# One explicit order of all TensorE units, scores, values and transposes in a fused attention and GEGLU kernel

## The chip, the cores and the metric

The kernel runs on one core of a Trainium2 chip. A core has five engines that work side by side: TensorE (PE, matrix products, with PEld for its weight loads), VectorE (DVE), ScalarE (ACT), GpSimd (POOL, which here issues the loads and casts them) and SyncE (SP, which issues stores and transposing transfers). The metric is the device time of the program in microseconds (us); the median of three runs of the kernel before is 404.07 us (403.4 to 404.55). The profile is of one execution, and its span runs from the first to the last instruction.

## The reference

Eight batches of 12 heads, 448 positions, 64 numbers a head: an attention with squared ReLU in place of the softmax, then a GEGLU block over the 3584 rows of 768 numbers that come out.

```python
scores = np.matmul(q, k.transpose(0, 1, 3, 2)) / np.sqrt(64)
attn = np.maximum(scores, 0.0) ** 2 / 448
x = np.matmul(attn, v)                    # to rows: (8 * 448, 12 * 64)
g, val = x @ w_gate, x @ w_val            # 768 -> 1536
out = (0.5 * g * (1 + erf(g / sqrt(2))) * val) @ w_out    # 1536 -> 768
```

## The kernel before

**Tiles.** The array is used as four tiles of 64 x 64. Each product is cut along its contraction in two: the lower half of it (operations named PE0 in the code) runs in one half of the array, the upper (PE1) in the other, and both add into the same bank of PSUM, one behind the other. So while one unit's upper half runs, the next unit's lower half runs beside it. A step is two matmuls of 64 rows and 64 columns over 448, 384 or 224 columns (`mm`, L365).

**Units.** A *score unit* (`add_scores`) makes two key chunks' scores in PSUM; ACT takes their ReLU (tile `rl`), and DVE squares two units at a time (`attnT`). A *value unit* (`add_values`, `ff<-attnT,v`) makes two heads' attention; DVE or ACT copies it to `xT`. A *gate* or *value product* (`add_gate_value`, `ff<-xT,wg` and `ff<-xT,wv`) makes 128 columns of the first FFN layer; ACT takes the gelu, DVE multiplies (`uT`). Part of the columns of batches 1 to 7 is made by seven products in place of eight, by Strassen's scheme as Winograd has it, as *pairs* (`add_pair`, over the sums `ts` of tokens and `ws` of weights, the latter made on DVE by `add_pair_sums`). The second FFN layer is done likewise for groups of rows (`add_product`, over `uT`, sums `s` of it, and sums `wt` of weights). *Transposes* of queries and keys are done on PE for batches 0 and 1 (`add_transposes`), and for batches 2 to 7 by a DVE copy (`qkr`) and two transposing transfers on SP for each third of a batch (`add_dma_transposes`).

**What sets the order.** The kernel is planned while it is built. `run_plan` takes the operations of every engine with a cost in us and what they wait for, and appends the next one that can start. Batch 0's attention has its own order (`START`), and everything on PE behind that start stands in a list of units sorted by a place in time (`later`). `next_unit` looks at the first 40 of them and takes the first that can start at once, or else the one that can start soonest; a score unit may also start inside another unit's run. ACT, DVE and SP take whatever is ready by priority. The order of each engine in the program is what comes out; the chip then runs each engine in order, with semaphores between them.

`LINE` gives the sequence of the FFN units: a digit is the next gate or value product of that batch, `2A6` is the product 6 of pair A of batch 2, `d7` is product 7 of row group d. The attention of batches 1 to 7 is not in it: each batch's score units, values and transposes are spread evenly between two places in time, which come from where the batch's FFN begins and two numbers a batch in `SHIFT`. The sums of pair weights go behind the last product that a rule names.

**Buffers that matter.** Scores use two bank pairs of PSUM at first; from a point on (`WIDE`) one is given to the FFN, and every score unit waits for the ReLU of the unit ahead of it. Loads of queries, keys and values on POOL wait for ReLUs and copies of earlier thirds (`PACE`), so they follow the order of scores. Transposing transfers wait for a mark in PE's order, one for each 256 PE instructions (`Blocks`, `gate`); stores behind row group 8 keep away from the edges of these blocks (`hold`).

Of the kernel before, what the change touches and what calls it, by code (L numbers as in the profile page):

```python
# [11 lines left out]
LINE = """  # L12
0 0 0 0 0 0 0 0 0 0 0 0 0 0 0 0 0 0 0 0 0 0 0 0 1 1A1 1 2 1A6 2 2 1 1A7 1A2 1A5 2 a1 2 a2 2A1 1A4 1
1 1 1A3 1 2 1 2A2 a6 1 2A7 a7 2 1 a5 1 1 2A6 2 2 1 1 1 1 a3 1 1 a4 1 1 b1 b7 c1 b2 b6 2A4 2 c6 b4 b5
c7 c5 2B1 2B6 c4 2B2 c3 b3 2A5 2 c2 2B7 2B4 2B5 2A3 2 3A1 2 3A2 2 2B3 2 2 3A6 3A7 d7 d1 3B1 d2 4C1
3B2 3 3C1 3B7 3 d6 3 e1 d4 3C7 3 3C6 3 3B6 e7 3B4 e6 3A4 3A5 3 3 3 3C2 3 3B5 3 3 d5 3C4 3A3 3C5 d3
4A1 4C2 3B3 3C3 e5 3 4A7 f1 f2 f6 e4 f7 4C7 4 e2 4C6 4A2 e3 g7 4B1 f5 4B6 4 4A6 4B2 g1 4B7 4 g2 4A5
4C5 4A4 4B4 4B5 f4 4D7 4D1 4C4 4 5B1 5 4D6 4D5 4A3 4 g6 4 g5 4C3 4B3 f3 4 5 5B2 4D2 4D4 g3 4D3 5C1
g4 5B6 5B7 5C2 5B5 5A1 4 5A6 5 5C7 5A7 5A2 5 5B4 5D1 h1 5A4 5D6 5D2 h6 5C6 h7 5 5D7 5D5 5A5 6A1 5B3
5 5C5 5C4 5A3 5C3 5D4 6B1 5 5D3 5 6A2 6B2 h4 i1 i2 6B7 6A6 i7 h5 6A7 h2 6D1 6F7 6D7 h3 j1 6D6 6C1  # L20
6D2 i6 j7 6E1 j6 6C7 6C2 6E7 i5 i4 6C6 6B6 6A5 6A4 6E6 6A3 6F1 6B4 6B5 6C5 6D5 6D4 6F6 i3 6B3 6F5
6C4 j5 6D3 6E2 6F2 6E5 6F4 6C3 6F3 6E4 6E3 7E7 j2 7E1 7B1 k1 k7 7E2 7A1 7B2 7B7 k2 7B6 7E6 j4 7C1 k6
7A2 l7 7C7 7C6 7A7 7B4 7C2 l1 7B5 7B3 k5 7A6 7F1 j3 7D1 7E5 7F7 7F2 7A5 k4 7F6 7E4 l6 7D7 7C4 7D2
7F4 7D6 7D5 7D4 7D3 l2 7F5 7A4 7C5 7C3 7E3 7A3 l5 l4 7F3 m1 n1 m7 k3 l3 m2 m6 n6 m5 n7 n4 m3 n5 n2
m4 n3
"""
# [5 lines left out]
"""  # L32


SHIFT = "-183 -79.5 40.75 1.75 -343.75 -112 43.75 -179.5 27.25 -513.5 -447.25 0.25"

# [59 lines left out]
class Unit:  # L96


    def __init__(self, at, los, his, box=None, closer=None, prev=None):
        self.at, self.los, self.his, self.box, self.closer, self.prev = at, los, his, box, closer, prev  # L100
        self.begun = False
        self.short = False


AHEAD = 40
BANK = 0.3


def run_plan(queues, pools, units, banks, arrivals, together, fill, blocks, span):

# [47 lines left out]
    def next_unit(short):  # L158
        best = None
        now = max(free["PE0"], floor)  # L160
        for u in units[:AHEAD]:
# [16 lines left out]
            if u.box is not None:  # L178
                k, end = None, None
                for n, c in banks.items():  # L180
                    x = 0.0 if c is None else c.end
                    if x is not None and (end is None or x < end):
                        k, end = n, x
                if k is None:
                    continue
                t = max(t, end + BANK)
            if short and t > now:
                continue
            t = max(t, now)
            if best is None or t < best[0]:  # L190
                best = (t, u, k)
                if t <= now:
                    break
# [5 lines left out]
    while left:  # L199
# [33 lines left out]
        if isinstance(op, tuple):  # L233
            _, u, k = op
            u.begun = True
            units.remove(u)
            if k is not None:
                u.box["k"] = k
                banks[k] = u.closer()
            queues["PE0"][at["PE0"]:at["PE0"]] = u.los  # L240
            pools["PE1"] += u.his
            op = u.los[0]
# [34 lines left out]
def kernel(  # L277
# [60 lines left out]
    mpool = ctx.enter_context(tc.tile_pool(name="mpool", bufs=RING_M))  # L338
    loaded = tc.tile_pool(name="lpool", bufs=2), tc.tile_pool(name="hpool", bufs=RING_H)
    lpool, hpool = (pool.__enter__() for pool in loaded)  # L340
# [125 lines left out]
    def add_dma_transposes(b, m, deps=()):  # L466
# [22 lines left out]
        n = len(regrouped)  # L489
        copy = Op("DVE", 0.62, emit_copy, [wait, *(regrouped[n - 2] if n > 1 else ())], lag=0.15, prio=1)  # L490
        DVE.append(copy)
# [93 lines left out]

    def then(at, step, los, his, box=None, closer=None):

        if not isinstance(at, list) and at > FIXED:
            his[0].deps.append(los[-1])
            for i, op in enumerate(his[1:]):  # L590
                op.after = his[i]
            later.append(Unit(at, los, his, box, closer))
            return
# [283 lines left out]
    def first_use(i):  # L877

        return min(b for b in range(B) if NPB[b] > i)
# [280 lines left out]
    def add_product(at, gr, name, final):  # L1160
# [103 lines left out]
        then(at, RS, *ops, box if name in opens else None, lambda: st["read", stages_last[stage]])  # L1264

# [36 lines left out]


    work = []
    flow = [[("g", b, fc, g) for fc in range(2 * NPB[b], FC) for g in range(2)] for b in range(B)]
    line = []
    for x in LINE.split():
        if len(x) == 1:
            line.append(flow[int(x)].pop(0))
        elif len(x) == 3:  # L1310
            line.append(("7", int(x[0]), "ABCDEFGHIJKL".index(x[1]), x[2]))
        else:
            line.append(("p", "abcdefghijklmn".index(x[0]), x[1]))
    assert not any(flow)
    at = 0.0
    starts = [None] * B
    placed = []
    for item in line:
        if item[0] == "g" and starts[item[1]] is None:
            starts[item[1]] = at  # L1320
        if item[0] == "7" and starts[item[1]] is None:
            starts[item[1]] = at
        placed.append((at, item))
        at += {"g": G, "7": G / 2, "p": R}[item[0]]
    starts.append(at)
    WIDE = 20.0
    for at, item in placed:
        if item[0] == "g":
            work.append((at, 5, add_gate_value, item[1:]))
        elif item[0] == "7":  # L1330
            work.append((at, 5, add_pair, item[1:]))
        else:
            _, gr, name = item
            work.append((at, 5, add_product, (gr, name, gr == B * SC // 4 - 1)))
    LEAD = 6.0

    LO1 = 2.0
    for b in range(B):
        if b == 0:
            lo, hi = -60.0, -12.0  # L1340
        elif b == 1:
            lo, hi = LO1, starts[1] - LEAD
        elif b == 2:
            lo, hi = starts[1] + 8.0, starts[2] - LEAD
        else:
            lo, hi = starts[b - 1] - LEAD, starts[b] - LEAD
        if b >= EARLY:
            lo, hi = lo + float(SHIFT.split()[2 * (b - 2)]), hi + float(SHIFT.split()[2 * (b - 2) + 1])
        if b >= EARLY:
            lo = max(lo, passed)  # L1350
            hi = max(hi, lo + 1.0)
        passed = hi
        step = (hi - lo) / NU
        if b < EARLY:
            for m in range(NM):
                for rs in ((0,), (1,)) if b == 0 else ((0, 1),):


                    x = -5.0 if m else -2.0
                    t_at = placed0[f"t{m}{rs[0]}"] if b == 0 else lo + SC * m * step + x  # L1360
                    if (b, m) == (1, 0):
                        t_at = PLACE5 + 0.05
                    work.append((t_at, 1, add_transposes, (b, m, rs)))
        for pr in range(NPAIR):
            u = SC * (pr // 2) + (VC - 1, SC - 1)[pr % 2]
            x = lo + u * step + max(4.5, 2.5 * step)
            if b == 0:
                x = placed0[f"v{pr}"] if pr < NPAIR - 1 else PLACE5
            work.append((x, 2, add_values, (b, pr)))
# [3 lines left out]
    for i in reversed(range(max(NPB))):  # L1373
        behind = [n for n, w in enumerate(work) if w[2] is add_gate_value and w[3][0] == first_use(i) - 1][-1]
        work.insert(behind + 1, (0.0, 5, lambda at, i: add_pair_sums(i), (i,)))


    for at, _, fn, args in work:
        fn(at, *args)
# [84 lines left out]
    banks = {k: readers.get(k, [None])[-1] for k in range(FB + 2)}  # L1464
    run_plan({"PE0": PE0, "POOL": POOL}, {"PE1": PE1, "ACT": ACT, "DVE": DVE, "SP": SP, "IDLE": IDLE}, later,
             banks, arrivals, ("PE0", "PE1"), fill, blocks, BLOCK)

# [29 lines left out]
```

## Time and profile before

| what | us |
|---|---|
| median of three runs (lowest, highest) | 404.07 (403.4, 404.55) |
| span of the profiled execution | 394.9 |
| outside the span (404.07 - 394.9) | 9.2 |
| PE busy, and 40 to 60 us into the span | 386.3, 20.00 of 20 |
| ACT busy | 258.7 |
| DVE busy | 309.6 |
| ReLU of one score unit on ACT | 0.919 |

The profiled execution has no time of its own beside its span, so the median stands for it. A row of instructions reads: line, engine, operation, out<-in by the program's names, shape, count, then busy time and mean time of one, then the engine's idle time ahead of them and what ended it. Idle time is given to the releaser that came last. PE's ends are modelled and its matmuls overlap, so that "busy" says only that some step was running.

### The profile page before, as it was taken

Reading aid. Unit: us, or ns where it says so; the run is one execution under the profiler, and the core shown is the slowest. Engines: PE = TensorE matmul, PEld = TensorE weight load, DVE = VectorE, ACT = ScalarE, POOL = GpSimd, SP = SyncE. Lnnn points to the kernel's source line nnn. Section 1 sums busy time; section 2 is a strip of 40 time slices with the busy share of each in tenths; the row PEclk is TensorE's granted clock in tenths of the full one; section 3 lists DMA queues with packets and bytes.
Section 4 is the critical chain, followed back from the end, with each engine's and each line's share of the span. In section 5 each row is a group of like instructions: output and inputs, shape, how many; then the busy total and the mean of one; then the engine's idle time right before and its main releaser. Section 6 shows DMA issues by size and latency. Waiting matters only on the chain.

```text
span 394.9 us, 22904 instructions
## 1 busy us (share of the span) xinstructions
PE 386.3 (98%) x10570; PEld 358.4 (91%) x10573; DVE 309.6 (78%) x522; ACT 258.7 (66%) x401; POOL 97.2 (25%) x156
## 2 busy tenths in 40 slices
PE   7999999999999999999999999999999999999995
PEld 3458889999999999999999999989999999999994
DVE  3885779968797499999797779758988999866772
ACT  5866872357677767787786478765787886535541
POOL 7656523322233323232332123310211000000000
PEclk9999999999999999999999999999999999999999
DMA  8999999988999969887999598880763501121134
GB/s 110 186 199 199 197 209 185 112 103 83 161 148 175 152 85 143 93 132 121 113 148 108 124 122 111 139 83 11 103 105 56 125 6 43 45 45 45 43 85 120
DMA packets 85567, 45.12 MB, mean 114 GB/s; under 512 B 46048, under 2 KB 82400, under 8 KB 85472
## 3 DMA queue, kind: packets, MB, share of 16 engines
q0 software_dynamic: 46944, 24.39, 49.9%
q1 hardware_dynamic: 37888, 18.49, 26.4%
q8 instruction: 82, 1.34, 1.4%
q10 hardware_dynamic: 640, 0.79, 0.6%
q14 instruction: 13, 0.11, 0.1%
HBM read 48.76 MB, written 11.01 MB: 151 GB/s over the span
## 4 chain that ended last, share of the span: by engine, by line
PE 93%; DVE 2%; DMA 2%; POOL 1%; issue 1%; ACT 0%; ACTq 0%; POOLq 0%
PE ff L365 85%; PE sp L365 7%; DMA qk<-in_k_dram 2%; DVE attnT L728 1%; PE sp L646 1%; POOL qk L424 1%; DVE xT L792 0%; PE ff L646 0%; ACTq L1241 0%; ACT osb L1225 0%; ACT rl L714 0%; PE ff L567 0%; DVE osb L1223 0%; DVE qkT L650 0%; POOL ident masks.py:199 0%
## 5 line engine op out<-in xcount | busy, mean ns | idle before, releaser
L714 ACT ACTIVATE rl<-sp 128x896 bf16<-128x896 f32 x168 | 152.1, 919 | 50.4 <-PE sp L365 45.1
L365 PE MATMUL ff<-xT,wg 64*64 64x224 bf16 (+1 forms) x2304 | 183.7, 299 | 0.6 <-issue 0.6
L365 PEld LDWEIGHTS <-wv 64*64 64x64 bf16 x2304 | 127.7, 107 | 4.4
L365 PEld LDWEIGHTS <-wg 64*64 64x64 bf16 x2304 | 123.3, 107 | 5.0 <-issue 0.5
L365 PE MATMUL ff<-xT,wv 64*64 64x448 bf16 x1056 | 120.8, 349 | 0.0
L728 DVE TENSOR_TENSOR attnT<-rl 128x1792 bf16<-128x1792 bf16 (+1 forms) x98 | 92.2, 952 | 6.6 <-ACT rl L714 6.2
L365 PEld LDWEIGHTS <-ws 64*64 64x64 bf16 x1872 | 92.3, 107 | 1.4 <-issue 1.0
L365 PEld LDWEIGHTS <-s 64*64 64x64 bf16 x1344 | 81.6, 107 | 1.8
L365 PE MATMUL ff<-attnT,v 64*64 64x448 bf16 (+1 forms) x768 | 79.7, 326 | 0.7 <-DVE attnT L728 0.6
L365 PE MATMUL ff<-ts,wv 64*64 64x224 bf16 x1248 | 78.7, 256 | 0.0
L365 PE MATMUL ff<-ts,ws 64*64 64x224 bf16 x1248 | 77.6, 256 | 0.0
L365 PE MATMUL sp<-qkT 64*64 64x448 bf16 (+1 forms) x768 | 74.6, 328 | 0.7 <-issue 0.3
L365 PE MATMUL ff<-wo,s 64*64 64x384 bf16 x672 | 63.4, 323 | 0.0
L966 DVE TENSOR_TENSOR part<-ff,part 128x448 f32<-128x448 f32 x78 | 47.5, 622 | 20.1 <-PE ff L365 16.4
L365 PEld LDWEIGHTS <-uT 64*64 64x64 bf16 x1008 | 62.5, 107 | 0.7
L365 PE MATMUL ff<-wt,s 64*64 64x384 bf16 x672 | 61.4, 322 | 0.0
L365 PE MATMUL ff<-wo,uT 64*64 64x384 bf16 x672 | 60.7, 322 | 0.0
L962 ACT COPY part<-ff 128x448 f32<-128x448 f32 x78 | 41.3, 534 | 12.4 <-PE ff L365 11.2
L443 POOL DMA_DIRECT2D v<-in_v_dram x48 | 29.6, 620 | 80.3 <-ACT rl L714 44.3
L365 PEld LDWEIGHTS <-v 64*64 64x64 bf16 x768 | 44.7, 107 | 4.1 <-issue 1.7
L424 POOL DMA_DIRECT2D qk<-in_q_dram x43 | 27.6, 642 | 80.0 <-ACT rl L714 59.5
L1049 DVE TENSOR_TENSOR uT<-gel,ff 128x448 bf16<-128x448 bf16 x44 | 27.3, 620 | 22.4 <-PE ff L365 11.0
(51 smaller groups left out, 423.9 us busy)
## 6 DMA issues: line engine op xcount, KB each, us to landing
out_dram<-osb SPq DMA_DIRECT2D x48, 192.0 KB, 3.3
v<-in_v_dram POOLq DMA_DIRECT2D x48, 128.0 KB, 4.1
wg<-in_moe_w_gate_dram POOLq DMA_DIRECT2D x6, 384.0 KB, 10.4
wv<-in_moe_w_val_dram POOLq DMA_DIRECT2D x6, 384.0 KB, 11.0
wo<-in_moe_w_out_dram POOLq DMA_DIRECT2D x4, 576.0 KB, 14.9
qk<-in_q_dram POOLq DMA_DIRECT2D x18, 128.0 KB, 3.5
qk<-in_k_dram POOLq DMA_DIRECT2D x18, 128.0 KB, 4.3
qk<-in_q_dram POOLq DMA_DIRECT2D x18, 96.0 KB, 3.8
```

The source lines that it names most:

```text
L365: ins = nc.tensor.matmul(o, lhsT, rhs, start=start, stop=stop, skip_group_check=onto, tile_position=(P * row, P * col))
L424: return nc.gpsimd.dma_start(qk16[b, m][HALF[i], r0:r0 + h1 - h0, cols], src[b, h0:h1].rearrange("h (p c) d -> p h (c d)", c=SC)[:, :, cols])
L443: return nc.gpsimd.dma_start(v16[b, m][HALF[i], h0 % 4:h0 % 4 + h1 - h0, :, :], v[b, h0:h1].rearrange("h (p c) d -> p h c d", c=SC)[:, :, ...
L646: blocks.add(nc.tensor.transpose(t[HALF[j], c, :], src[:, 2 * r + j, c, :], ident[:, :], tile_position=(0, P * j)))
L714: relu.ins = nc.scalar.activation(duo["rl"][:, u % 2, :, :], box[0][:, :, 0:S], AF.Relu).ins
L728: nc.vector.tensor_tensor(a[:, part], duo["rl"][:, part], duo["rl"][:, part], op=ALU.mult)
L962: rd.ins = nc.scalar.copy(st["t", name][:, :], box[0][:, 0:S]).ins
L966: rd.ins = nc.vector.tensor_tensor(t[:, :], box[0][:, 0:S], t[:, :], op=ALU.add).ins
L1049: u_op[b, fc].ins = nc.vector.tensor_tensor(uT[b][:, fc, :], gel.pop((b, fc))[:, :], box[0][:, 0:S], op=ALU.mult).ins
```

## The change

`LINE` now holds every unit behind the start, one mark each: `s` is the next score unit, `v` the next values, `t` the next transposes on PE (batch 1), `w3` the sums of pair weights 3, and the other marks are as they were. `SHIFT` and the rules that spread the attention between two places are gone. Each mark's place in the planner's list is its number in `LINE`; the first two products of batch 0, batch 0's attention and batch 1's first transposes stay where they were. The spare score bank is given to the FFN when 44 score units stand, in place of a time. The look ahead over 40 units stays, so the list is a priority and the program's order may differ from it in places.

`Unit`, `then` and `run_plan` learn to take a second bank for a unit (`more`, with a map `full` of banks and a cost `COVER`). No unit asks for one. The number of regrouped tiles gets a name, `RING_L`, and stays 2. If the pair sums never closed the pools of loads, they are closed at the end.

```diff
 LINE = """
-0 0 0 0 0 0 0 0 0 0 0 0 0 0 0 0 0 0 0 0 0 0 0 0 1 1A1 1 2 1A6 2 2 1 1A7 1A2 1A5 2 a1 2 a2 2A1 1A4 1
...
-7F4 7D6 7D5 7D4 7D3 l2 7F5 7A4 7C5 7C3 7E3 7A3 l5 l4 7F3 m1 n1 m7 k3 l3 m2 m6 n6 m5 n7 n4 m3 n5 n2
-m4 n3
+0 0 s s t s s s s s s s t s s s s v v s v s s s s v s s s v 0 0 s s v 0 0 0 0 0 s 0 0 s 0 0 0 0 1A1
+v 1A2 0 0 1 s s s w0 s 0 1A6 1A7 1 a7 s s s s s s s s s 1 1 1 1 1 1 1 1 0 0 0 s 1 1 1A5 v v 2A1 v v
...
+l4 7E4 l3 7F7 7D7 7D4 7D5 7F5 7B5 7B3 7F2 7F4 7D3 7E3 n1 7F3 n6 m1 m7 m6 m4 n7 m2 n4 n5 n2 n3 m5 m3
 """
-SHIFT = "-183 -79.5 40.75 1.75 -343.75 -112 43.75 -179.5 27.25 -513.5 -447.25 0.25"
...
+            k2 = None
+            if u.more is not None:
+                for n, c in banks.items():
+                    x = 0.0 if c is None else c.end
+                    if n != k and n in full and x is not None and (k2 is None or x < end):
+                        k2, end = n, x
...
+    RING_L = 2
...
-        if at > WIDE and n % SB == 0 or wide:
+        if n >= WIDE and n % SB == 0 or wide:
...
-        if b >= EARLY:
-            lo, hi = lo + float(SHIFT.split()[2 * (b - 2)]), hi + float(SHIFT.split()[2 * (b - 2) + 1])
...
-        step = (hi - lo) / NU
...
-        for u in range(NU):
-            work.append((placed0[f"s{u}"] if b == 0 else lo + u * step, 3, add_scores, (b, u)))
-    work.sort(key=lambda w: w[:2])
...
+    flow_s = [(b, u) for b in range(1, B) for u in range(NU)]
+    flow_v = [(b, pr) for b in range(1, B) for pr in range(NPAIR)]
+    flow_t = [(1, m, (0, 1)) for m in range(1, NM)]
...
+    for n, x in enumerate(LINE.split()):
+        at = 1.0 + n
+        if x[0] == "w":
+            work.append((0.0, lambda at, i: add_pair_sums(i), (int(x[1]),)))
+        elif x == "s":
+            work.append((at, add_scores, flow_s.pop(0)))
+        elif x == "v":
+            work.append((at, add_values, flow_v.pop(0)))
+        elif x == "t":
+            work.append((at, add_transposes, flow_t.pop(0)))
...
+    WIDE = 44
```

More of the change, by code (lines that the diff above doesn't have):

```diff
@@ new lines @@
+2 a3 b1 b6 s s s s s w2 c1 s c6 s s s b2 s b4 b5 s s b3 s v s s v v c7 c5 c4 c3 c2 v 2 2 s 2 2B2 2 2
+2B7 2 2B6 2B4 v v 2 s 2 3B1 s s s 2 2 v s s s d1 d2 2B5 2 2 3A1 2B3 2A3 d6 s 3 3B2 3A2 d7 3A6 3B7
+3A7 3B6 s s s 3 d4 3B5 v v v 3 d5 3C1 3 3 3C7 3B4 3B3 3A4 s s s s s s s s 3A5 s s s 3C2 3 3 e1 3C6
+3C5 d3 v 3 s 3C4 3C3 e2 e6 4A1 e7 e5 v s e3 s s 4A2 4A7 v 4C1 3A3 e4 3 3 v 4A6 4A4 3 3 s f1 s s s f2
+4A5 4A3 s f6 4C7 s s s s v 4C2 f7 f5 s s s 4C6 4B1 4B2 4 4 4 4 s s 4B6 4C4 s v s s w3 4B7 4B5 4B4 s
@@ new lines @@
+s s s 4D1 4C5 4C3 4D7 v g1 f4 4D6 4D5 g6 g2 f3 4 4 v v 4D2 g7 4 5B1 g5 g3 g4 s s 4D4 4D3 4 5B6 5C1
+5C6 5C2 5C7 5 5 5 4B3 s s s s 5B2 5B7 5B5 s s 5A1 s s s 5 5C5 5A6 5B4 5B3 5 v s h1 v 5A7 h6 v v h2 s
+v 5A2 5 5C4 5C3 5D1 s 5D6 5D2 5A4 h7 s s s s s s s s s s 5D7 5 5 w5 5A5 6B1 5D4 h4 h5 5D5 5D3 6B7
+6B6 s s s s 6A1 6B2 6A7 i1 6B4 5A3 i7 6B5 i6 h3 s i2 6A2 v 6C1 i5 i4 6B3 i3 6D1 6D2 6D6 6C6 v 6C2
+6A6 6A5 s j1 6A4 6A3 6D7 v v 6C7 6C4 w4 6C5 6C3 6F7 6F1 s 6D5 6F2 s 6F6 j7 6E1 6D4 6E2 s 6F5 6E7 6E6
@@ L26 @@
+6E4 j2 7B1 v s 6E5 6F4 6F3 v 7E7 7E1 7E2 j6 j5 j4 k7 k1 7B2 7A1 7A2 7A6 k2 7A7 7A4 6E3 7B7 l1 7C1
+7C2 7C7 6D3 k6 7E6 j3 l6 7C6 l7 7D1 7D2 k5 k4 7F1 7B6 7E5 7B4 7F6 7C5 7A5 7D6 l5 k3 7C4 7C3 7A3 l2
+l4 7E4 l3 7F7 7D7 7D4 7D5 7F5 7B5 7B3 7F2 7F4 7D3 7E3 n1 7F3 n6 m1 m7 m6 m4 n7 m2 n4 n5 n2 n3 m5 m3
 """
@@ L96, with __init__ @@
 class Unit:
-    def __init__(self, at, los, his, box=None, closer=None, prev=None):
+    def __init__(self, at, los, his, box=None, closer=None, prev=None, more=None, full=True):
         self.at, self.los, self.his, self.box, self.closer, self.prev = at, los, his, box, closer, prev
+        self.more, self.full = more, full
         self.begun = False
@@ L106, with run_plan @@
 BANK = 0.3
-def run_plan(queues, pools, units, banks, arrivals, together, fill, blocks, span):
+COVER = 0.06
+def run_plan(queues, pools, units, banks, full, arrivals, together, fill, blocks, span):
     free = {e: 0.0 for e in (*queues, *pools)}
@@ L186, in next_unit @@
                 t = max(t, end + BANK)
+            k2 = None
[4 more added lines that the diff above has]
+                        k2, end = n, x
+                if k2 is None:
+                    continue
+                t = max(t, end + BANK)
             if short and t > now:
@@ L190, in next_unit @@
             if best is None or t < best[0]:
-                best = (t, u, k)
+                best = (t, u, k, k2)
                 if t <= now:
@@ L233, in run_plan @@
         if isinstance(op, tuple):
-            _, u, k = op
+            _, u, k, k2 = op
             u.begun = True
@@ L239, in run_plan @@
                 banks[k] = u.closer()
+                full[k] = u.full
+            if k2 is not None:
+                u.more[0]["k"] = k2
+                banks[k2] = u.more[1]()
+                if not full[k2]:
+                    u.more[0]["cover"] = True
+                    u.los[0].cost += COVER
+                full[k2] = True
             queues["PE0"][at["PE0"]:at["PE0"]] = u.los
@@ L489, in add_dma_transposes @@
         n = len(regrouped)
-        copy = Op("DVE", 0.62, emit_copy, [wait, *(regrouped[n - 2] if n > 1 else ())], lag=0.15, prio=1)
+        copy = Op("DVE", 0.62, emit_copy, [wait, *(regrouped[n - RING_L] if n >= RING_L else ())], lag=0.15, prio=1)
         DVE.append(copy)
@@ L584, in both, with then @@
             pairs.append(("with", lo, hi))
-    def then(at, step, los, his, box=None, closer=None):
+    def then(at, step, los, his, box=None, closer=None, more=None, full=True):
         if not isinstance(at, list) and at > FIXED:
@@ L591, in then @@
                 op.after = his[i]
-            later.append(Unit(at, los, his, box, closer))
+            later.append(Unit(at, los, his, box, closer, None, more, full))
             return
@@ L1263, in add_product @@
                 reads_u.setdefault(b, []).append(ops[1][-1])
-        then(at, RS, *ops, box if name in opens else None, lambda: st["read", stages_last[stage]])
+        then(at, RS, *ops, box if name in opens else None, lambda: st["read", stages_last[stage]], full=False)
     for h0, h1 in ((0, 2), (2, 4), (4, 8), (8, 12)):
@@ L1301 @@
         add_dma_transposes(b, m)
+    flow = [[("g", b, fc, g) for fc in range(2 * NPB[b], FC) for g in range(2)] for b in range(B)]
+    flow_s = [(b, u) for b in range(1, B) for u in range(NU)]
+    flow_v = [(b, pr) for b in range(1, B) for pr in range(NPAIR)]
+    flow_t = [(1, m, (0, 1)) for m in range(1, NM)]
     work = []
[L1305 to L1309, printed above, removed]
+    for x in START.split():
+        at = placed0[x.rstrip("a")]
+        n = int(x.rstrip("a")[1:])
+        if x[0] == "t":
+            work.append((at, add_transposes, (0, n // 10, (n % 10,))))
+        else:
+            work.append((at, {"s": add_scores, "v": add_values}[x[0]], (0, n)))
@@ new lines @@
+    work.append((PLACE5, add_values, (0, NPAIR - 1)))
+    work.append((PLACE5 + 0.05, add_transposes, (1, 0, (0, 1))))
+    for g in range(2):
+        work.append((0.0, add_gate_value, flow[0].pop(0)[1:]))
+    for n, x in enumerate(LINE.split()):
[8 more added lines that the diff above has]
+            work.append((at, add_transposes, flow_t.pop(0)))
+        elif len(x) == 1:
+            work.append((at, add_gate_value, flow[int(x)].pop(0)[1:]))
@@ L1310 @@
         elif len(x) == 3:
-            line.append(("7", int(x[0]), "ABCDEFGHIJKL".index(x[1]), x[2]))
+            work.append((at, add_pair, (int(x[0]), "ABCDEFGHIJKL".index(x[1]), x[2])))
         else:
[L1313 to L1346, printed above, removed]
-        if b >= EARLY:
-            lo, hi = lo + float(SHIFT.split()[2 * (b - 2)]), hi + float(SHIFT.split()[2 * (b - 2) + 1])
[L1349 to L1352, printed above, removed]
-        step = (hi - lo) / NU
[L1354 to L1369, printed above, removed]
-        for u in range(NU):
-            work.append((placed0[f"s{u}"] if b == 0 else lo + u * step, 3, add_scores, (b, u)))
@@ L1372 @@
-    work.sort(key=lambda w: w[:2])
[L1373 to L1378, printed above, removed]
+            gr = "abcdefghijklmn".index(x[0])
+            work.append((at, add_product, (gr, x[1], gr == B * SC // 4 - 1)))
+    assert not any(flow) and not flow_s and not flow_v and not flow_t
@@ L1379 @@
+    WIDE = 44
+    for at, fn, args in work:
         fn(at, *args)
@@ L1464 @@
     banks = {k: readers.get(k, [None])[-1] for k in range(FB + 2)}
+    full = {}
     run_plan({"PE0": PE0, "POOL": POOL}, {"PE1": PE1, "ACT": ACT, "DVE": DVE, "SP": SP, "IDLE": IDLE}, later,
-             banks, arrivals, ("PE0", "PE1"), fill, blocks, BLOCK)
+             banks, full, arrivals, ("PE0", "PE1"), fill, blocks, BLOCK)
+    if not rest:
+        for pool in loaded:
+            pool.__exit__(None, None, None)
 _INS = ['q', 'k', 'v', 'moe_w_gate', 'moe_w_val', 'moe_w_out']
```

13 lines of the change are left out of this document (2 added, 11 removed).

## Prediction

> **What bounds the kernel now.** I read the page's first part and its chain of waits, then the busy time by stretches, then TensorE's own waits, then single instructions in time order.
>
> ```profile
> span 394.9 us, 22904 instructions
> PE 386.3 (98%) x10570; PEld 358.4 (91%) x10573; DVE 309.6 (78%) x522; ACT 258.7 (66%) x401; POOL 97.2 (25%) x156
> PE 93%; DVE 2%; DMA 2%; POOL 1%; issue 1%; ACT 0%; ACTq 0%; POOLq 0%
> ...
> 0.00:20.00 20.00, 17.06 (x217) 8.69 (x221) 11.34 (x22) 13.85 (x18) 13.89 (x26) 1.00 1.09 149
> 20.00:40.00 20.00, 19.14 (x373) 13.66 (x372) 13.96 (x24) 12.71 (x18) 12.00 (x17) 1.00 1.39 199
> 40.00:60.00 20.00, 20.00 (x441) 16.89 (x435) 14.70 (x20) 15.32 (x21) 7.57 (x11) 1.00 1.33 203
> ...
> 260.00:280.00 20.00, 19.35 (x633) 18.75 (x627) 15.61 (x27) 12.70 (x25) 1.84 (x3) 1.00 0.49 51
> ...
> 380.00:400.00 20.00, 10.73 (x247) 9.69 (x236) 5.24 (x12) 2.76 (x6) 0.00 (x0) 0.90 0.30 80
> ```
>
> In a row of the second kind stand the stretch, then the busy time of PE, PEld, DVE, ACT and POOL, the granted clock, and DMA. PE is busy all of every 20 us from 40 us on, but for 0.65 us in 260 to 280 and the tail; the clock there is 1.00. Outside the span lie 404.07 - 394.9 = 9.2 us, which no order of units touches. The waits of PE and of its weight loads between 34 and 388 us, in full:
>
> ```profile
> PE ff L365 <- issue: 0.6, 1, 0.6
> ...
> PEld L365 <- issue: 1.5, 4, 0.8
> PEld L646 <- issue: 0.4, 1, 0.4
> ```
>
> So for 354 us PE never waits on ACT, DVE or a transfer, and once on its own instructions. The only thing that an order can still change in that stage is how well its steps fit together:
>
> ```profile
> 44.47 0.35 PE L365 MATMUL ff<-xT,wg 64*64 64x448 bf16 x2
> 44.56 0.35 PE L365 MATMUL ff<-attnT,v 64*64 64x448 bf16 x2
> 44.66 0.35 PE L365 MATMUL ff<-xT,wg 64*64 64x448 bf16 x2
> 44.75 0.35 PE L365 MATMUL ff<-xT,wv 64*64 64x448 bf16 x2
> ...
> 304.59 0.38 PE L365 MATMUL ff<-attnT,v 64*64 64x448 bf16 x2
> 304.78 0.54 PE L365 MATMUL ff<-ts,wv 64*64 64x224 bf16 x7
> 305.07 0.38 PE L365 MATMUL sp<-qkT 64*64 64x448 bf16 x2
> ```
>
> A row names one step of two matmuls in one half of the array. At 44 us two halves alternate: each starts a 448-column step every 0.19 us (44.47 to 44.66, 44.56 to 44.75). At 304.8 us one half works alone for 0.29 us (304.78 to 305.07), in which half of the array's work is lost. A busy PE hides such stretches.
>
> **The change part by part.** *Work.* The built programs have the same 10,573 matmuls and weight loads, 400 ACT operations, 522 of DVE, and the same loads, transposes and stores. The new arguments of the unit and of the planner (a second bank, its cover) have no caller, the ring of two regrouped tiles has two as before, and both orders open the spare score bank at batch 1's end. Removed and added work: 0 us. What moves is where units stand.
>
> *Start.* The two instruction orders are identical up to this score, the first one of batch 1:
>
> ```profile
> 29.74 0.51 PE L365 MATMUL sp<-qkT 64*64 64x448 bf16 x4
> 18.33 7.52 ACT L714 ACTIVATE rl<-sp 128x896 bf16<-128x896 f32 x9 [0.34 <-PE sp L365]
> ```
>
> There a step of batch 0's gate product comes first, then this score. Thus the stretch that is thinnest (PE 17.06 of 20, and ACT's nine ReLUs end to end until 25.85) stays as it was: 0 us. Behind it batch 1's scores come a little denser: counted in PE work, its last score starts at 43.4 us of it, was 45.6. The first loads are issued in the same sequence, the weights of the next products are used at the same place or later, and DMA is full in that stage either way (1.33 to 1.39). I take 0 for it; the bounds are a gain of the 0.86 us that PE idles between 20 and 40 us, and a loss as large.
>
> *Pairing.* I counted in both built orders, at the 0.19 us per 448 columns above, how long one half of the array has no partner even if nothing is waited for: 8.9 us before, 7.1 us after. The start (the same) and the last product (1.1 us in both) hold most of it; what goes are short stretches at five places of the middle, the one at 304.8 us among them. A step without a partner wastes half the array, so (8.9 - 7.1) / 2 = 0.9 us. No other work hides it, since PE sets the end all through. Bounds: 0.5 us (half of the new pairs slip apart) and 1.1 us.
>
> *The one stall.*
>
> ```profile
> 264.60 0.87 PE ff L365 x37
> 265.47 0.65 issue
> 266.12 10.41 PE ff L365 x282
> ...
> 260.00:264.00 4.00, 4.00 (x147) 3.83 (x141) 2.48 (x5) 3.89 (x9) 0.61 (x1) 1.00 1.34 92
> 264.00:268.00 4.00, 3.35 (x135) 3.17 (x128) 1.85 (x4) 1.32 (x3) 0.00 (x0) 1.00 0.13 21
> ...
> q8 instruction: 82, 1.34, 1.4%
> ...
> 250.06 34.75 SPq L480 DMA_TRANSPOSE qkT<-qkr  x5
> ```
>
> "issue" is a wait that the profile shows no releaser for; the DMA share was 1.34 just before it (queries, keys and transposes at once), and the program is itself fetched by DMA: 82 transfers, 1.34 MB, 16 KB each. I read the stall as a late fetch. Transposes start at a mark in the PE order, so a new order puts them against other fetches. Bounds: no stall (0.65 us gained) or, with one stall in each of three such crowded places, 1.3 us lost. I take 0.5 us gained, nearer the first end: only one of 36 transposes did this, and around PE's 250th us the new marks lie further apart.
>
> [...]
>
> *ACT and DVE.*
>
> ```profile
> L714 ACT ACTIVATE rl<-sp 128x896 bf16<-128x896 f32 x168 | 152.1, 919 | 50.4 <-PE sp L365 45.1 <-DVE attnT L728 2.8 <-ACT part L962 0.7
> L728 DVE TENSOR_TENSOR attnT<-rl 128x1792 bf16<-128x1792 bf16 (+1 forms) x98 | 92.2, 952 | 6.6 <-ACT rl L714 6.2
> ```
>
> From batch 2 on one score bank is left, so a score unit waits for the ReLU of the one before it: 0.92 us. Between the end of one unit and the start of the next the old order has at least 1.12 us of PE work, the new one 1.27 us. For each stretch of 10 us of PE work I added up what it hands to ACT and DVE at the rows' durations: behind the start ACT gets up to 9.8 us (10.6 before), DVE over 11 us in three stretches (seven before). So I see no new wait: 0 us, bounds in the rivals.
>
> *Transposes.* The closest transfer is batch 2's first:
>
> ```profile
> 69.94 0.62 DVE L475 COPY qkr<-qk 128x1792 bf16<-128x1792 bf16 x1
> ...
> DMA to landing us min/median/max: 2.7/4.6/7.2
> ...
> 81.59 0.13 PE sp L365 x3
> ```
>
> Copy to score is 11.65 us and PE showed no wait. The new order has 0.8 us less work between them (10.0 against 10.8), but releases the second of the two transposes 0.8 us sooner behind the copy. I take 0; with two transposes end to end at median and longest, 0.62 + 4.6 + 7.2 = 12.4 us, 1.5 us would be lost. The other thirds have 8.9 us or more behind their last transpose's release. On SP the transposes stand ahead of stores, and POOL's loads wait for ReLUs at about the same PE work as before.
>
> *Tail.*
>
> ```profile
> 388.35 2.38 PE L365 MATMUL ff<-wo,s 64*64 64x384 bf16 x36
> 389.79 0.48 ACT L1225 COPY osb<-ff 128x384 f32<-128x384 f32 x1 [4.55 <-PE ff L365]
> 390.84 0.48 ACT L1225 COPY osb<-ff 128x384 f32<-128x384 f32 x1 [0.57 <-PE ff L365]
> ```
>
> Both orders end with the same four kinds of product, two ACT copies and the same split stores: 0 us.
>
> *Sum.* 394.9 - 0.9 - 0.5 = 393.5 us of span; with 9.2 us outside it 402.7, against 404.07.
>
> **The rivals.** (1) *The fit improves, the time doesn't.* The stall stays or comes elsewhere and half of the pairs slip: 404.07 - 0.5 = 403.6; between 403.0 and 404.9. For it: fetches and transposes cross anew, and 0.9 us is little. Against: PE's order is fixed in the program, and nothing made it slip before. (2) *ReLUs come late.* ACT takes its instructions in order; where the new order puts gelu or copies (0.5 us) ahead of a ReLU, the next score waits, and with it all of PE behind it. Price: 0.02 us for each of 125 scores is 2.5 us, 404.07 - 0.9 + 2.5 = 405.7. It decides from about 17 ns a score (2.1 us) on. For it: ReLUs are ACT's largest group. Against: 1.27 us is more room than the 1.12 that the old order lives with. (3) *More is gained.* Denser batch 1 also takes the 0.86 us between 20 and 40 us: 402.7 - 0.9 = 401.8. Against: that idle time is mostly ahead of the first difference. (4) *The change doesn't do what it says*, the planner rebuilding the old order: excluded, since the built order differs from 29.74 us on.
>
> **How the numbers follow.** Forecast 402.7 with chance 0.48 (its own range 402.0 to 403.4); rival 1: 0.27; rival 2: 0.15; rival 3: 0.10. The bound for a change is 0.3%, 1.2 us: 402.86 and 405.28. Faster: three fifths of the forecast's 0.48, all of rival 3 and some of rival 1, 0.43. Slower: rival 2 and a late transpose, 0.15. Between them 0.42. The range reaches down into rival 3 and up over rival 2: 401.2 to 405.8.
>
> **What would show it.** Right: a span near 393.5, PE's waits between 34 and 388 us of 1 us or less, no "issue" of 0.65 us, and no stretch with one half alone near 304 us. Wrong: rows "PE sp" waiting for ACT rl (rival 2), "PE sp" for a transpose at about 80 us, or several "issue" pieces on the chain (rival 1).

## The result and the profile after

The changed kernel took 402.81 us (median of 22 runs, 399.96 to 407.23), the kernel before, run beside it, 400.83 us (median of 22). The medians lie 2.0 us apart. The ratio, with the executions that count as slow left out, is 1.006, 95% interval 1.0037 to 1.0082: 0.6% slower, or 2.4 us. The number forecast, 402.7, is almost the number measured, but only because the three times of before that were shown (403.4 to 404.55) lie high among the 22 (396.91 to 404.55). The forecast was 1.4 us faster; the change made it slower.

The page of the kernel after, its span, engines, transfer queues and chain of waits:

```profile
span 400.2 us, 22901 instructions
PE 389.6 (97%) x10570; PEld 358.2 (90%) x10573; DVE 310.8 (78%) x522; ACT 260.5 (65%) x401; POOL 97.0 (24%) x156
...
q8 instruction: 82, 1.34, 1.5%
...
PE 92%; DMA 3%; DVE 2%; ACT 1%; issue 1%; ACTq 0%; POOL 0%; POOLq 0%
```

All that PE and its weight loads waited for between 34 and 390 us, after (engine, line and what it waited for: us in total, times, longest):

```profile
PE ff L385 <- issue: 2.1, 6, 0.9
PE sp L385 <- DMA qkT<-qkr: 1.1, 1, 1.1
PE ff L385 <- PE ff L385: 0.2, 1, 0.2
PEld L385 <- issue: 7.3, 12, 1.4
PEld L385 <- DVE qkT L670: 0.4, 1, 0.4
PEld L666 <- issue: 0.4, 1, 0.4
```

Before, PE had one "issue" of 0.6 us here, and its weight loads 1.5 and 0.4 us of it. After, PE is as good as always busy still (97%), the chain is still PE, and no ReLU is waited for. What is new are many more small holes for which the profile names no releaser (2.1 us of PE, 7.3 and 0.4 of its weight loads; the two overlap in time), a wait for a transpose, and one for VectorE's copy of batch 1's transposed tile.

The time of this run was 401.96 us, 1.8 us above its span. So the first profile of before (394.9 us) is hardly one of an execution of 404 us. The two profiles to hand are then a short execution of one kernel and a middling one of the other, and no fair pair. The first experiments repeat both.

### The profile page after: what moved, and what is told of

Same layout as the page of the kernel before. It is cut to its first block, busy times and chain, and to the rows that moved or that the text cites. A ratio compares the mean times of both kernels' runs of the same rounds, so it can differ in the third digit from the quotient of the medians.

```text
span 400.2 us, 22901 instructions
## 1 busy us (share of the span) xinstructions
PE 389.6 (97%) x10570; PEld 358.2 (90%) x10573; DVE 310.8 (78%) x522; ACT 260.5 (65%) x401; POOL 97.0 (24%) x156
## 3 DMA queue, kind: packets, MB, share of 16 engines
q8 instruction: 82, 1.34, 1.5%
## 4 chain that ended last, share of the span: by engine, by line
PE 92%; DMA 3%; DVE 2%; ACT 1%; issue 1%; ACTq 0%; POOL 0%; POOLq 0%
PE ff L385 82%; PE sp L385 8%; DMA qkT<-qkr 2%; DVE attnT L748 1%; ACT rl L734 1%; DMA qk<-in_k_dram 1%; PE sp L666 1%; PE ff L587 0%; DVE xT L812 0%; PE ff L666 0%; ACT osb L1245 0%; PE ff L629 0%; DVE qkT L670 0%; ACTq L1261 0%; POOL qk L444 0%
## 5 line engine op out<-in xcount | busy, mean ns | idle before, releaser
L385 PEld LDWEIGHTS <-wv 64*64 64x64 bf16 x2304 | 129.0, 107 | 5.9 <-issue 1.5
L385 PEld LDWEIGHTS <-wg 64*64 64x64 bf16 x2304 | 126.7, 107 | 5.6 <-issue 1.4
L385 PEld LDWEIGHTS <-ws 64*64 64x64 bf16 x1872 | 95.4, 107 | 2.0 <-issue 1.5
L385 PE MATMUL ff<-attnT,v 64*64 64x448 bf16 (+1 forms) x768 | 84.2, 326 | 0.7 <-DVE attnT L748 0.6
L385 PE MATMUL sp<-qkT 64*64 64x448 bf16 (+1 forms) x768 | 78.4, 329 | 1.6 <-DMA qkT<-qkr 1.1
L385 PE MATMUL ff<-wo,s 64*64 64x384 bf16 x672 | 65.2, 323 | 0.2 <-PE ff L385 0.2
L385 PE MATMUL ff<-wo,uT 64*64 64x384 bf16 x672 | 64.3, 323 | 0.0
L385 PEld LDWEIGHTS <-v 64*64 64x64 bf16 x768 | 46.5, 107 | 4.1 <-issue 2.1
L385 PEld LDWEIGHTS <-qkT 64*64 64x64 bf16 x768 | 39.0, 106 | 7.3 <-issue 4.3
```

What stands on the lines that cost most here:

```text
L385: ins = nc.tensor.matmul(o, lhsT, rhs, start=start, stop=stop, skip_group_check=onto, tile_position=(P * row, P * col))
```

## The experiments

**A measure for them.** For each matmul I took its start in a profile less the start that it would have in the built order if nothing were waited for (0.19 us per 448 columns in each half of the array). Where this difference grows, PE waited or ran slower than that. Without waits the old order is 376.75 us long, the new one 375.83: 0.9 us less, which is the better pairing. The profile also dates every matmul, so a hole can be numbered by the count of PE instructions (matmuls and weight loads) ahead of it.

**Both kernels profiled again.** before2 is the kernel before, after2 and after3 the kernel after. before3 is the changed code with the old order in it:

```
-LINE = """0 0 s s t s s s s s s s t s s s s v v s v s ...
+LINE = """0 0 ... (the order of the kernel before, its scores, values and transposes written out too)
```

Of before2: 

> The kernel before, profiled once more. Theory F (the loss is fetches of the program that arrive late and differ from one execution to the next; the first profile of before, 394.9 us, was an early one): a span of 398 to 400 us, 1.7 to 2 us below its own time, and 2 to 4 us of gaps between matmuls behind 34 us, all at multiples of 256 PE instructions, where the first profile had 1.4. Theory P (the first profile is typical, and 9.2 us lie outside the span): a span near 395 us and one such gap over 0.5 us.

Of before3: 

> The changed code, planner and all, with the old order written into it: the instruction sequence of every engine is that of the kernel before. If the order alone makes the difference: ratio 1.000 (0.998 to 1.002), and a profile like the kernel before's. If something else in the change did (code, pools, ring): a ratio near 1.006.

Of after2: 

> The changed kernel once more. Ratio 1.004 to 1.008. Theory F: gaps at multiples of 256 PE instructions, 5 us or so in sum, of which those between 41 and 66 us come back and single ones behind them move or vanish. Theory T (batch 2's second transfer of transposes lands late, a fixed loss of the new order): PE's first score of batch 2, at 82 to 84 us, waits 1.0 to 1.5 us for it again.

Of after3: 

> The changed kernel a third time. As for the second: T expects the wait of 1.0 to 1.5 us at 82 to 84 us in each profile; F expects gaps at the multiples of 256 PE instructions in each, with sizes that differ by 1 us or more in sum between profiles.

Measured: before2 401.18 us with a span of 398.1, 3.1 us below it, so more lies outside than I expected. before3 0.9996 (0.9962 to 1.0029): the code around the order costs nothing that shows within 0.3%, so the order alone makes the difference. after2 1.0079 (1.0046 to 1.0112). after3 401.9 us of span, 403.7 of time. The waits of PE in the same window, of before2 and of before3, one fence each:

```profile
PE ff L365 <- issue: 0.7, 2, 0.5
PE sp L365 <- DMA qkT<-qkr: 0.3, 1, 0.3
PE sp L365 <- ACT rl L714: 0.3, 1, 0.3
PEld L365 <- issue: 4.6, 12, 0.7
PEld L646 <- issue: 0.4, 1, 0.4
```

```profile
PE ff L385 <- issue: 3.2, 5, 0.9
PEld L385 <- issue: 6.1, 12, 1.1
PEld L666 <- issue: 0.4, 1, 0.4
```

The old order has holes too, most of them others in each profile: from its 300th matmul on it lost 4.4, 7.5 and 8.7 us by the measure above, the new order 10.4, 10.0 and 12.6. The first profile of before was the luckiest of the three. Theory P falls. What tells the orders apart is what comes back in all three profiles of one order. Taking for each 100 matmuls the least of the three, the old order loses 2.7 us every time, the new one 6.1. The extra 3.4 us less 0.9 for the pairing makes 2.5 us, against 2.4 measured. The match is looser than that: a hole lengthens the span, and the median spans of this set of runs lie 3.4 us apart (397.9 and 401.3), so about 0.9 us is left to holes that differ from one execution to the next. The times lie only 2.9 us apart (400.21 and 403.11), since less lies outside the new order's span.

Theory T falls as well. The new order's waits at batch 2's first score, 79 to 86 us, are in its first profile

```profile
PE sp L385 <- DMA qkT<-qkr: 1.1, 1, 1.1
```

and none is named in after2 and after3. It is a matter of chance: before2 has 0.3 us of it too.

The holes that come back in the new order, as the time from one start of a matmul to the next (0.19 us or less is usual), in ns, by the PE instructions counted ahead of them in the first profile (a few records more or less in the others; "-" is under 230). A hole of 279 ns at batch 1's transposes, which both orders have in every profile, is left out:

```
PE instruction  at us  after  after2  after3
           916   34.7    350     349     349
          1716   53.4    530     530     530
          1972   59.4    305     305     305
          2228   65.3    865     865     865
          5554  134.1    425     840     772
          8110  181.6    540     451       -
         10410  222.6    289     289     837
         11688  245.5   1237     552     788
```

All but the first stand 256 instructions, or a multiple of them, apart, if one allows for the few records that a trace lacks (their remainders fall from 180 to 168). Program comes in pieces of 16 KB (82 pieces, 1.34 MB, in the row of q8), which for the 10,570 matmuls and 10,573 weight loads of the page is 258 to a piece. The first hole, at 34.7 us, is the 0.4 us for VectorE's copy qkT. The third early one, to the nanosecond the same in three executions, in the first profile's timeline:

```profile
65.28 0.38 PE L385 MATMUL ff<-xT,wv 64*64 64x448 bf16 x2 [0.52 <-issue]
```

in after2's:

```profile
64.55 0.38 PE L385 MATMUL ff<-xT,wv 64*64 64x448 bf16 x2 [0.52 <-issue]
```

and in after3's:

```profile
64.50 0.38 PE L385 MATMUL ff<-xT,wv 64*64 64x448 bf16 x2 [0.52 <-issue]
```

**Less to transfer.** If the holes are program that comes late because other transfers are ahead of it, they must go when there is less to transfer. The same instructions on every engine, but loads of one head instead of four:

```diff
+            few = 1 if b >= EARLY else h1 - h0
             return nc.gpsimd.dma_start(
-                qk16[b, m][HALF[i], r0:r0 + h1 - h0, cols],
-                src[b, h0:h1]...
+                qk16[b, m][HALF[i], r0:r0 + few, cols],
+                src[b, h0:h0 + few]...
```

and so for values; a third whose load is cut takes over the buffer of the third that had it last. These kernels leave out three heads of four, so their output isn't the reference's. The second pair has `b >= 1` in place of `b >= EARLY` (EARLY is 2).

> The new order, but the loads of queries, keys and values of batches two to seven (counted from nought) carry one head of four; the rest of the buffers keeps what was in them, so the output isn't the reference's. Every engine has the same instructions in the same order. Theory F (program fetches late behind other transfers): the gaps at block boundaries that all three profiles of the new order have behind 100 us (near 133, 181, 222 and 245 us) shrink under 0.3 us each; those between 34 and 66 us, where only weights and earlier batches are loaded, stay at 1.5 us or so in sum. Time 399 to 400.5 us, ratio 0.997 to 1.001. Theory O (the new order loses on TensorE itself or on ACT and DVE, whatever the transfers): ratio 1.005 to 1.008, as before.

> The same lightening of loads in the old order (output not the reference's). F: only the gaps that differ from profile to profile vanish, so less is gained than in the new order: 398 to 399.5 us, ratio 0.995 to 0.998; the difference of the two orders falls from 2.7 us to about 1.0 us (1.9 us lost before 70 us, less the 0.9 us of better pairing). O: the difference stays at 2.4 us or more.

> As the lightened new order, with batch one's loads (issued at 28 to 37 us, among the weights) cut to one head of four as well; the output isn't the reference's. Theory F for the early stage (while the transfers are full, 28 to 65 us, a block of 256 PE instructions can't be had in less than about 6 us, and the new order's blocks are shorter than that): the full stage ends by about 53 us, the gaps of 305 and 865 ns at 59 and 65 us vanish and that of 530 ns shrinks; 0.7 to 1.1 us less than with batches two to seven lightened alone (397.5), so 396.4 to 396.8 us. Rival E (these gaps are fixed in TensorE's own instructions): they stay to the nanosecond, 397.5 us.

> The same in the old order, whose early gaps are 40 ns or so each: F expects 397.8 to 398.1 us, within 0.3 us of the first lightening (398.1), and so a new order that is 1.0 to 1.7 us faster than the old once fetches are on time. E: a difference of 0.6 us as with the first lightening.

Measured:

| loads cut from | old order | new order | ratio to the kernel before, old / new |
|---|---|---|---|
| none | 400.21 (23 runs) | 403.11 (12 runs) | 1 / 1.0079 (1.0046 to 1.0112) |
| batch 2 | 398.08 (12 runs) | 397.52 (9 runs) | 0.9923 (0.9888 to 0.9958) / 0.9901 (0.9869 to 0.9933) |
| batch 1 | 396.95 (6 runs) | 396.58 (6 runs) | 0.9894 (0.9853 to 0.9934) / 0.9877 (0.984 to 0.9914) |

The rows are from three chips, each with its own runs of the kernel before, so the ratios are what compares across rows: the first cut gains the new order 1.8% (1.0079 to 0.9901), the old one 0.8%. Within each row the two orders ran on the same chip, and they turn round: 2.9 us slower becomes 0.6 and 0.4 us faster. These last two lie within their intervals, so what they show is that the 2.9 us are gone, not that the new order is ahead: by the medians of the spans it goes from 3.4 us behind to 0.25 and 0.15 us ahead (395.95 and 395.7, 394.95 and 394.8), and the rest lies outside the spans. Both orders gained more from the first cut than I expected (0.9901 against 0.997 to 1.001, and 0.9923 against 0.995 to 0.998), and the new order, expected 1.0 us behind there, is level. With the second cut the old order came out below its range too (396.95 us against 397.8 to 398.1), so the second pair's 0.4 us falls short of the 1.0 to 1.7 us that I expected. Theory O falls. Waits of PE alone, without those of its weight loads, from 34 to 390 us with loads cut from batch 2, new order:

```profile
PE ff L385 <- issue: 1.2, 3, 0.5
```

and with loads cut from batch 1 as well, new order:

```profile
PE ff L385 <- issue: 0.2, 1, 0.2
```

The weight loads of the new order still show 3.5 and 2.1 us of "issue" in these two profiles (7.3, 7.1 and 9.9 with all loads), those of the old order 2.0 and 0.3.

The holes at 181, 222 and 245 us are gone with the first cut, as expected; the one at 133 us stayed in one of the two profiles (414 ns). The early three stayed with the first cut (529, 305 and 865 ns); the transfers are nearly as full there as without it (210 GB/s at 52 to 56 us and 190 at 60 to 64, against 209 and 207). With the second cut the 865 ns went, the other two stayed (529 and 305), so that the new order's 396.58 us fell into its range (396.4 to 396.8) in part by luck. Not as expected: the full stage ended at about 58 us and not at 53, so the fetches for both of these still fell into it. The transfers in three stretches (the last three columns are granted clock, DMA share and GB/s), after:

```profile
56.00:60.00 4.00, 4.00 (x94) 3.54 (x90) 3.80 (x7) 1.46 (x2) 0.72 (x2) 1.00 1.16 211
60.00:64.00 4.00, 4.00 (x108) 3.45 (x102) 2.36 (x6) 1.20 (x3) 1.12 (x2) 1.00 1.20 207
64.00:68.00 4.00, 3.48 (x100) 2.89 (x93) 3.35 (x6) 1.52 (x3) 1.83 (x3) 1.00 1.45 184
```

and with loads cut from batch 1:

```profile
56.00:60.00 4.00, 4.00 (x96) 3.54 (x91) 3.80 (x7) 1.46 (x2) 1.71 (x4) 1.00 0.70 97
60.00:64.00 4.00, 4.00 (x104) 3.47 (x98) 2.36 (x5) 1.05 (x2) 0.17 (x1) 1.00 0.21 23
64.00:68.00 4.00, 4.00 (x123) 3.70 (x116) 4.00 (x8) 1.90 (x4) 0.00 (x0) 1.00 0.02 4
```

PE's busy time in the last row of each goes from 3.48 to 4.00: that is the hole of 0.52 us. The starts of the program's fetches (packets of q8 in the trace) say why:

```
after:                  44.81  50.99  57.08  62.91  67.69  71.21
loads cut from batch 1: 45.18  51.28  57.48  60.81  64.51  70.64
```

While the transfers are full, one fetch starts 5.8 to 6.2 us behind the other; as soon as they aren't, the next two follow in 3.3 and 3.7 us, less than the 5.1 us of PE work in the shortest block here, so it isn't PE that sets the pace in the full stage. (The one behind them, 6.1 us later, is no longer waited for.) PE goes on 2.3 to 2.5 us behind the start of a fetch that it waited for (62.91 to 65.28, 50.99 to 53.44). Between the three early holes lie 5.92 us each (53.44, 59.36, 65.28). Without waits PE needs for the 256 instructions ahead of the second 5.58 us in the new order, ahead of the third 5.11, and 5.68 and 5.96 in the old. So the new order loses 5.92 - 5.58 = 0.3 and 5.92 - 5.11 = 0.8 us there, and the old one 0.2 us at the first and nothing at the second, since its steps there are longer. The old order meets the same pace: in its first profile these boundaries stand at 52.68, 58.60 and 64.52 us, 5.92 us apart too, and at the first two its weight loads wait for nothing that the profile names:

```profile
52.68 0.10 PEld L365 LDWEIGHTS <-wg 64*64 64x64 bf16 x1 [0.26 <-issue]
```

```profile
58.60 0.10 PEld L365 LDWEIGHTS <-wg 64*64 64x64 bf16 x1 [0.23 <-issue]
```

Behind 82 us a block is 4.35 us of PE work on the average. PE's groups between 47 and 66 us, by shape, of before2 (line, output and inputs, shape, count; busy us, mean ns; idle before):

```profile
L365 PE MATMUL ff<-xT,wv 64*64 64x448 bf16 x156 | 17.8, 349 | 0.0
L365 PE MATMUL ff<-xT,wg 64*64 64x448 bf16 x149 | 17.5, 349 | 0.0
...
L365 PE MATMUL ff<-attnT,v 64*64 64x224 bf16 x18 | 2.5, 256 | 0.0
L365 PE MATMUL sp<-qkT 64*64 64x224 bf16 x8 | 0.4, 256 | 0.0
```

and of after2:

```profile
L385 PE MATMUL ff<-xT,wg 64*64 64x448 bf16 x136 | 15.3, 350 | 0.0
L385 PE MATMUL ff<-xT,wv 64*64 64x448 bf16 x122 | 14.0, 350 | 0.7 <-issue 0.7
...
L385 PE MATMUL ff<-xT,wg 64*64 64x224 bf16 x48 | 3.0, 256 | 0.0
...
L385 PE MATMUL ff<-ts,ws 64*64 64x224 bf16 x12 | 0.8, 256 | 0.0
L385 PE MATMUL ff<-ts,wv 64*64 64x224 bf16 x7 | 0.5, 256 | 0.0
```

The new order brings 67 short matmuls of the pair products (48 + 12 + 7 of 224 columns, two to a step) into this stage, the old one none: more instructions for the same PE time, just where program is scarce (5.92 us for a block).

**Moving the boundaries alone.** Transposes are started at marks in the PE order that the planner sets by counted instructions. Some more, uncounted instructions in the warm-up move the block boundaries against the marks, and nothing else:

```diff
-        for _ in range(8):
+        for n in range(24):            # 40, 56
             for j in range(2):
-                blocks.add(nc.tensor.matmul(t[HALF[j], :], warm[:, HALF[j]], warm[:, :], ...))
+                ins = nc.tensor.matmul(t[HALF[j], 0:171], warm[:, HALF[j]], warm[:, 0:171], ...)   # 102, 73
+                if n < 8:
+                    blocks.add(ins)
```

> The new order, with the warm-up of TensorE cut into 32 more matmuls of as many columns in all, which the planner doesn't count: 64 more PE instructions, so each block boundary of 256 instructions falls 64 instructions earlier in the order, while transposes and stores start at the same matmuls as before. F: every gap now lies 64 PE instructions (32 matmuls) earlier in the order, sizes behind 100 us change, and the time moves by 0.5 us or more either way (401 to 405 us). O, and T (late transposes): the losses stay at the same matmuls, 402.5 to 403.5 us.

> As pad64, with 128 more PE instructions: boundaries fall half a block earlier, and transposes start in the middle of a block instead of about its beginning. F: gaps 128 PE instructions earlier in the order, and more of them, as a fetch now has a running transpose in its way: 403.5 to 407 us, ratio 1.008 to 1.017. O and T: 402.5 to 403.5 us.

> The new order with 192 more PE instructions in the warm-up (block boundaries 192 earlier, which is 64 later in the cycle of 256). F: all gaps at multiples of 256 again, at new places of the order; the sum is what decides, 401 to 406 us. If the new order's own loss is only a bad fit of phases, one of the three shifts should come out at or below the kernel before (400 to 401 us).

> The old order with the same 128 more PE instructions as in the new order's second shift, which cost that one 3 us. F: it costs the old order as much or more, 403 to 406 us, since the old order has no more room between fetches and transposes than the new. If the old order were robust against late fetches by its arrangement: 400 to 401.5 us.

Measured: 64 more, 402.69 us (1.0036, 1.0004 to 1.0068); 128 more, 406.11 (1.0104, 1.0043 to 1.0165); 192 more, 408.56 (1.0195, 1.0145 to 1.0246); the old order with 128 more, 406.64 (1.0144, 1.0097 to 1.0191). The first lies in the ranges of both theories, so there the places of the holes must decide; the last two came out above what I expected (401 to 406 and 403 to 406 us). PE's waits from 34 to 390 us with 128 more, new order:

```profile
PE ff L385 <- issue: 6.9, 11, 1.9
PEld L385 <- issue: 11.8, 18, 2.2
```

and old order, where a transpose also came late:

```profile
PE ff L365 <- issue: 3.1, 5, 1.5
PE sp L365 <- DMA qkT<-qkr: 1.0, 1, 1.0
...
PEld L365 <- issue: 9.2, 16, 1.9
```

The holes of the new order with 64 and 128 more stand at the counts 1719, 2231, 5557, 8623 (and others 256 apart), on the grid of the count and so at matmuls 32 and 64 earlier in the order; the one of 0.4 us for qkT stayed with its matmul (351 ns at 983 and 1047, which is 64 and 128 behind the 919 of the runs with cut loads). That tells late program from late data and from the marks, and E, under which the early holes belong to TensorE's own instructions, falls with it. Theory F stands. How much is lost hangs on where the marks lie against the boundaries, in both orders: of the four places tried for the new order, as built and with 64 more are best, of the two for the old one, as built. No shift brought the new order below the old as built. With 64 more, less was lost late (3.9 us behind the 4000th matmul, against 4.3 to 6.8 in three profiles of the new order as it is), and more early (6.0 us from the 300th to the 1500th, against 3.5 to 4.2), where holes of 1.3 and 1.6 us came at 46.7 and 70.9 us, the second put down to VectorE's sum wt for 1.3 us of it.

By stages, in us lost against the order without waits, from the single profiles:

| matmuls (of 10573) | 300 to 1500 | 1500 to 4000 | 4000 to the end |
|---|---|---|---|
| old order, three profiles | 1.9, 2.0, 2.5 | 0.1, 1.8, 0.2 | 2.4, 3.7, 6.0 |
| new order, three profiles | 3.7, 3.5, 4.2 | 2.1, 2.2, 1.6 | 4.6, 4.3, 6.8 |
| loads cut from batch 2, old / new | 1.9 / 3.3 | 0.1 / 0.6 | 2.8 / 2.2 |
| loads cut from batch 1, old / new | 1.6 / 2.7 | 0.1 / 0.4 | 1.3 / 1.8 |
| new order, 64 / 128 / 192 more | 6.0 / 3.6 / 3.9 | 0.3 / 3.4 / 2.2 | 3.9 / 8.0 / 9.7 |
| old order, 128 more | 2.5 | 2.5 | 6.7 |

## Why the prediction was wrong

- *What bounds the kernel, and 9.2 us outside the span.* PE sets the end: right. The 9.2 us were wrong: they joined the span of one execution to the median of three others. Run by run, 1.7 to 2.1 us lie outside the new order's span, and 1.9 to 4.4 outside the old one's in the runs of these experiments, never 9. From 394.9 us of span and these the old order would take 396.8 to 399.3 us, so 404.07 was the time of other, longer executions. Spans tell the two orders apart better than times do: 397.9 to 398.9 us (medians of the old on three chips) against 401.1 and 401.3 (two medians of the new).
- *Work and start.* No work was added: before3 agrees. For batch 1 I took 0, with 0.86 us either way, since "DMA is full in that stage either way". This is the first step that failed, and the larger one. While DMA was full, program was scarce (5.92 us for a block, and with batch 1's loads cut fetches 3.3 and 3.7 us apart as soon as it wasn't), and the denser steps ran into that: 0.3 and 0.8 us at 59 and 65 us, and 0.3 at 53 us (530 - 190 ns). Another 0.4 us is a score that now comes before VectorE has copied qkT (34.7 us). By the least of three profiles this stage (300th to 1500th matmul) costs the new order 1.7 us more. The profile to hand could have told: the row of weight loads that the prediction shows (1.5 us of "issue", four times) holds the two waits at 52.68 and 58.60 us, 0.5 us of the 1.5, and the prediction made nothing of them.
- *Pairing.* 0.9 us less PE work without waits is what the built orders have. No run shows it by itself: once the loads are light, the new order is ahead by 0.25 and 0.15 us of span, which can't be told from nothing, and in the single profiles it still loses 1.3 and 1.9 us more than the old by the measure above. So the term may be right; it is given back nearly four times over (3.4 us).
- *The one stall.* Read rightly as a late fetch, and sized wrongly: I took 0.5 us gained from a single profile that had one such stall, with 1.3 us lost as the worst. The stall at 266 us came back at the same boundary in before2 (755 ns between starts, at 267.8 us) and in no profile of the new order, so its part was a gain. But at four other boundaries behind 100 us (133, 181, 222, 245 us) the new order loses 1.4 us in every execution (0.4, 0.2, 0.3 and 0.5, the least of three), and chance adds to it in either order. The 82 pieces for 10,570 matmuls and 10,573 weight loads, 258 to a piece, agree with the grid of the holes, 256. Most of the pieces cost nothing that the waits show (6 of PE and 13 of its weight loads are "issue" in the first profile of the new order, 34 to 390 us), but not enough of them: holes came back at six boundaries in all three profiles and cost up to 1.0 us each (1237 - 190 ns).
- *ACT and DVE, rival 2.* No row of PE waiting for a ReLU in the three profiles of the new order: right to leave it at 0.
- *Transposes.* I took 0 with 1.5 us as the bound: 1.1 us in the first of the three, none named in the others. Chance, not the order.
- *Tail.* 0.2 us more lost in the last 180 matmuls of the new order in each profile; the cause is open.
- *Rivals.* Rival 1 named the mechanism (fetches and transposes cross anew, several "issue" pieces) and priced it at 403.0 to 404.9 from the wrong base; taken against the old order it never left room for a loss of 2.4 us. The side "slower" got its 0.15 from ReLUs and transposes, not from fetches.

What stays open: which transfer holds up each late fetch behind 100 us (cutting loads removed the holes, but loads and transposes run together there), why a little less lies outside the new order's span, what the better pairing is worth on the chip, and whether a version exists that keeps it without the holes. Of the twelve kernels run for these experiments, none beat the kernel before with the whole work done.

## What to carry to other kernels

Here TensorE was the bound, with 21,143 matmuls and weight loads in 400 us, and its program was itself a transfer, 82 pieces of 16 KB. In such a kernel count instructions per us against the rate at which blocks of program arrive while transfers are full (here 256 in 5.92 us). The denser order wasn't better where program was scarce (0.3 and 0.8 us lost at 59 and 65 us). Placing big transfers where the steps are long may then help; no run here tried it. Profile both kernels several times ahead of reading a difference of 1%: here the holes that came back in each profile were the order's (6.1 us of the new one's 10.0 to 12.6), the rest was chance.

## What was not expected of the hardware

- A late fetch in the full stage costs the same to the nanosecond in every execution (305, 530 and 865 ns, three times each), and within 1 ns of it with the later loads lightened (529, 305 and 865 ns): so the rate of program there looks set, not random. Behind it the same boundary differs from one execution to the next (1237, 552 and 788 ns at 245 us).
- A piece of 16 KB that takes 0.9 to 1.0 us on its queue lets PE go on 2.3 to 2.5 us behind its start.
- Executions of one kernel with the whole work spread by 4 to 8 us (396.91 to 404.55 for the old order), and the three profiles of the old order differ by as much (4.4 to 8.7 us lost) in such holes.
